# A third batch's gate stores moved ahead of the first expert's weight loads, in a kernel of causal attention and a mixture of experts

## The chip, the cores and the metric

The kernel runs as one program on one core of a Trainium2 chip. The metric is its device time in microseconds (us), the median of several runs; lower is better. Matrix products run on TensorE (PE; its weight loads are listed as PEld), element-wise work on VectorE (DVE), ScalarE (ACT) and GpSimd (POOL), and SyncE (SP) issues most of the DMA transfers. All inputs are float32 in DRAM.

## The reference

Causal attention over 4 batches, 12 heads, 448 positions and a head size of 64 gives 1792 rows ("tokens") of 768 numbers. Each token then goes through one of 8 experts, the one with the largest logit, and the result is scaled by that expert's softmax probability, the gate.

```python
scores = q @ k.T / sqrt(64)              # per batch and head, 448 x 448
attn = softmax(where(causal, scores, -1e9))
x = (attn @ v) rearranged to [1792, 768]
logits = x @ w_gate                      # [1792, 8]
e = argmax(logits, 1)
gate = softmax(logits)[token, e]
out = gate * (relu(x @ w1[e]) @ w2[e])   # w1 768 x 1024, w2 1024 x 768
```

## The kernel before

**Attention.** The work is cut into 24 pairs of heads, six to a batch. `step(p)` (L301) is one turn of a software pipeline written out by hand: it computes the scores of pair p+1 (`scores`, whose evacuation with the mask and the row minimum is VectorE's L151), their exponentials (`exps`, ScalarE), the transposes of pair p's probabilities (`transposes`), the value products of pair p-1 (`values`, whose last call copies the result from PSUM to a tile xt, L215), and `back(p-2)`. `back` multiplies xt with an identity and the pair's gate weights on TensorE (L247), scales the two heads' results by the reciprocal row sums on VectorE (L250, four products: x and its part of the logits, lgp, for each head) and stores the 128 columns of x to xd in DRAM (L227, L228, issued by SyncE). xd has 1792 rows of 784 numbers: 768 of x and 16 with the gate of the token.

**Routing.** When a batch's last pair has gone through `back`, `route(b)` (L278) is queued. It is a generator: `drip` (L263) advances it between the calls of a step, only at places that its last `yield` names; `at(j, f)` stands for the place behind call j of f. It sums the logits on GpSimd (L345 to L348), takes the maximum, computes `ex`, the exponentials of the logits, on ScalarE (L282), ranks the tokens of each expert with two small products (`rank`), turns ranks into places (`places`), and adds up a table `ids` of token numbers by expert and place (`tally`, L432). `gates(b)` (L365) turns the sum of `ex` into the gate `pre` and stores it into the last 16 columns of xd.

**Experts.** The expert stage works in 18 slots of 128 tokens of one expert. The third batch (b = B - 2) is special: its routing chooses the experts of the first three slots from three batches' tokens alone, so that the expert stage can start while the last batch's attention still runs. `top_slot` (L448) finds the expert with most tokens; SyncE reads its number (L504) and issues the eight loads of its weights (`load_raw`, L642, 768 KB each: u 0 to 3 are w1, 4 to 7 are w2). `early_slots` (L508) picks the first slot's token numbers (`pick`, L626, the cast of `idx` at L630 on GpSimd) and gathers their rows from xd (`gather`, L656, an indirect DMA on GpSimd; for an early slot it reads xd[0:1344], the first three batches). It then chooses the experts of slots 2 and 3 with small operations on VectorE and fills their entries of a table on GpSimd. The end of `route` reads the entries' numbers into registers, picks both slots' tokens and gathers the second slot's rows.

**The weights** are split into a high part (ScalarE, L695) and a low part (VectorE, L701) by `split_parts`, which then loads the next slot's part into the same buffer, or notes it as owed where that slot's expert isn't known yet. `x_turn(s)` (L720) transposes a slot's rows (TensorE, L730) and splits them too; `first` and `second` are the two products.

**The order around the change.** The calls of a step stand in `pos`; the last pair's, where the first slot's splits and transposes are mixed with the last attention work, stand in a list of their own (L1012 to L1019). Ahead of it `drip(1000)` (L1009) runs all of the routing that is left. Each engine works through its instructions in the order in which they are written, and SyncE's transfers go through one queue.

```python
def drip(n=1, at=None, among=None):
    while n and todo:
        if at and at not in (want[0] or among):
            return
```

Of the kernel before, what the change touches and what calls it, by code (L numbers as in the profile page):

```python
# [14 lines left out]
ALU = mybir.AluOpType  # L15
# [8 lines left out]
NCH = 4  # L24
# [55 lines left out]
def attention_moe_kernel(ctx: ExitStack, tc: tile.TileContext, qk_in, v_in, wi_in, w1, w2, c_in, out):  # L80
# [149 lines left out]
    def back(p):  # L230
# [17 lines left out]
        for h in (1, 0):  # L248
            for dst, lo, n in ((X[p][:, :, h], 0, D), (LG[b][:, :, 2 * pr + h], D, E)):
                nc.vector.tensor_tensor(  # L250
                    out=dst, in0=both[h][:, :, lo:lo + n],
                    in1=rs[:, :, h:h + 1].to_broadcast([C, NCH, n]), op=ALU.mult,
                )
# [9 lines left out]
    def drip(n=1, at=None, among=None):  # L263
        while n and todo:
            if at and at not in (want[0] or among):
                return
            try:
                want[0] = next(todo[0])
                n -= 1
            except StopIteration:  # L270
                todo.pop(0)
                want[0] = None
# [5 lines left out]
    def route(b):  # L278
# [3 lines left out]
        nc.scalar.activation(gt[b]["ex"], gt[b]["lg"], ACTF.Exp)  # L282
        yield at(NCH - 1, values) if b == B - 2 else at(0)
# [10 lines left out]
        if b == B - 2:  # L294
            yield from early_slots()
            for i in range(1, EARLY):
                load_regs(i)
                pick(i)
# [66 lines left out]
    def gates(b):  # L365
        g = gt[b]
        V.tensor_scalar_add(g["sm"], g["sm"], 1e-9)
# [10 lines left out]
    def places(b):  # L378
# [10 lines left out]
        V.tensor_reduce(out=g["sm"], in_=g["ex"], axis=AX.X, op=ALU.add)  # L389
# [22 lines left out]
        if b == B - 2:  # L412
            yield
            gates(b)
# [33 lines left out]
    def top_slot():  # L448
# [14 lines left out]
        def top(n, i):  # L463

            V.tensor_reduce(out=u[f"m{i}"], in_=n, axis=AX.X, op=ALU.max)
            V.scalar_tensor_tensor(out=t["eq"], in0=n, scalar=u[f"m{i}"], in1=e8_1, op0=ALU.is_equal, op1=ALU.mult)
            yield
            V.tensor_reduce(out=u[f"e{i}"], in_=t["eq"], axis=AX.X, op=ALU.min)

        def rest(n, i):  # L470
            V.tensor_scalar(out=t[f"o{i}"], in0=e8_1, scalar1=u[f"e{i}"], scalar2=None, op0=ALU.is_equal)
            yield
            V.scalar_tensor_tensor(
                out=t[f"n{i + 1}"], in0=t[f"o{i}"], scalar=float(-4 * NT), in1=n, op0=ALU.mult, op1=ALU.add
            )

# [20 lines left out]
        early["all"] = n, t, u, tf, top, rest, plus, entry  # L497
        yield from top(n, 0)
# [9 lines left out]
    def early_slots():  # L508
        n, t, u, tf, top, rest, plus, entry = early["all"]
        pick(0)  # L510
        gather(0)
        yield
        yield from rest(n, 0)
        yield from top(t["n1"], 1)
        yield from rest(t["n1"], 1)
        yield from top(t["n2"], 2)
        V.tensor_scalar(out=u["c1"], in0=u["m0"], scalar1=256.0, scalar2=None, op0=ALU.is_lt)
        V.tensor_scalar(out=u["c2"], in0=u["m0"], scalar1=384.0, scalar2=None, op0=ALU.is_lt)
# [448 lines left out]
    with tc.manual_schedule():  # L967
# [41 lines left out]
        drip(1000)  # L1009
        p = NP - 1  # L1010
        del plan[:2]
        for f, *a in [  # L1012
            (transposes, p, 0), (transposes, p, 1), (recips, p - 2), (back, p - 2), (split_parts, 0, (0,), ("low",)),
            (split_parts, 0, (1,), ("high",)), *((values, p - 1, kc) for kc in range(NCH)),
            (transposes, p, 2), (transposes, p, 3), (recips, p - 1), (back, p - 1), (split_parts, 0, (2,), ("high",)),
            (x_turn, 0), *((values, p, kc) for kc in range(NCH)), (split_parts, 0, (1,), ("low",)),
            (split_parts, 0, (3,), ("high",)), (first, 0, 0, 0), (split_parts, 0, (2,), ("low",)), (recips, p),
            (back, p), (split_parts, 0, (3,), ("low",)),
# [112 lines left out]
```

## Time and profile before

| | us |
|---|---|
| median of 3 runs | 515.77 |
| lowest and highest of them | 515.5, 517.25 |
| the profiled execution, its own time | 517.6 |
| span in that profile | 515.8 |
| TensorE busy | 490.8 (95% of the span) |
| TensorE weight loads busy | 403.0 (78%) |
| VectorE busy | 309.2 (60%) |
| ScalarE busy | 299.4 (58%) |
| GpSimd busy | 120.7 (23%) |
| mean granted clock of TensorE | 0.975 of full |

The profile is one execution, taken by the hardware profiler, with times in us from the start of its span. Its page gives busy time by engine and in 40 slices of 12.9 us, with the granted clock in tenths. The other views read the trace: the timeline lists an engine's work in order, neighbours of one kind taken together, and in brackets the idle time before and what ended it; the waits add up idle time by what was waited for; the windows give busy time, clock and DMA traffic of a stretch. A matrix product's end is modelled, and a wait for several things is put down to the one that came last.

### The profile page before, as it was taken

What the parts mean: (1) busy time and instruction counts of PE and PEld (TensorE: products, weight loads), DVE (VectorE), ACT (ScalarE), POOL (GpSimd) and SP (SyncE); (2) the same over time, 40 slices, a digit from 0 to 9 for tenths busy, and PEclk for the clock granted to TensorE, in tenths of its full rate; (3) what the DMA queues carried; (4) which work ended last, traced back from release to release, by engine and by line L of the source; (5) the groups of instructions that cost most, each with busy time, mean ns of one, the idle gap of its engine ahead of it and who ended that gap; (6) DMA issues with size and microseconds to landing.
All of it is one profiled execution on the core that took longest, in us unless ns stands there. A gap on an engine that the chain in (4) does not pass through costs nothing. (4 is left out here: it accounts for less than half of the span.)

```text
span 515.8 us, 10948 instructions
## 1 busy us (share of the span) xinstructions
PE 490.8 (95%) x3242; PEld 403.0 (78%) x3242; DVE 309.2 (60%) x872; ACT 299.4 (58%) x669; POOL 120.7 (23%) x200
## 2 busy tenths in 40 slices
PE   8999999999999489999999999999999999999973
PEld 5677766677666358989988988988899889878863
DVE  4777887787889549511025356367454314895773
ACT  6988877878778425122146347464753335775651
POOL 2000123114012164521033013113530111444201
PEclk9999999999999869999999999999999999999995
DMA  8355544445537740011382592585734257977630
GB/s 267 124 149 149 149 136 116 145 135 147 148 95 286 242 121 28 4 63 50 122 254 86 202 350 77 193 319 196 280 141 156 69 188 268 320 269 244 236 124 17
DMA packets 46327, 85.89 MB, mean 167 GB/s; under 512 B 5674, under 2 KB 18090, under 8 KB 46256
## 3 DMA queue, kind: packets, MB, share of 16 engines
q1 hardware_dynamic: 42944, 73.74, 43.2%
q0 software_dynamic: 2880, 11.13, 6.2%
q8 instruction: 29, 0.48, 0.4%
q14 instruction: 42, 0.34, 0.2%
q10 hardware_dynamic: 432, 0.20, 0.2%
HBM read 138.45 MB, written 12.70 MB: 293 GB/s over the span
## 5 line engine op out<-in xcount | busy, mean ns | idle before, releaser
L701 DVE TENSOR_TENSOR lo<-raw,hi 128x1536 fp32r<-128x1536 f32 x64 | 110.6, 1759 | 8.4 <-ACT hi L695 3.4
L163 ACT ACTIVATE s<-s,nm 66x64 f32<-66x64 f32 (+1 forms) x192 | 95.7, 501 | 21.2 <-DVE nm L151 21.1
L695 ACT CAST hi<-raw 128x1536 fp32r<-128x1536 f32 x64 | 93.7, 1485 | 9.0 <-ACTq L693 2.7
L759 ACT COPY hs<-l 128x512 f32<-128x512 f32 x36 | 21.2, 588 | 115.5 <-PE l L757 114.6
L770 PE MATMUL l<-hi,xh 128*128 128x512 f32 x216 | 86.8, 402 | 0.0
L151 DVE CUSTOM_DVE_ANT_0 s<-ps,cs 66x64 f32<-66x64 f32 (+1 forms) x192 | 70.0, 418 | 5.1 <-PE ps L145 5.0
L860 PE MATMUL y<-lo,hh 128*128 128x384 f32 x280 | 72.6, 341 | 0.1
L775 PE MATMUL l<-lo,xh 128*128 128x512 f32 x180 | 71.0, 394 | 0.6
L855 PE MATMUL y<-hi,hh 128*128 128x384 f32 x250 | 64.6, 340 | 0.4
L732 DVE TENSOR_TENSOR xl<-xT,xh 128x384 fp32r<-128x384 f32 x36 | 18.5, 552 | 76.2 <-ACT xh L731 76.1
L791 DVE SCALAR_TENSOR_TENSOR hl<-hT,hh 128x512 fp32r<-128x512 f32 x28 | 19.3, 689 | 64.8 <-ACT hh L788 36.7
L145 PE MATMUL ps<-qk 64*66 64x64 f32 (+3 forms) x384 | 56.1, 398 | 0.9 <-DVE nm L151 0.7
L863 POOL DMA_INDIRECT out<-y,idx x16 | 26.2, 1639 | 113.9 <-ACTq L693 72.3
L860 PEld LDWEIGHTS y<-lo,hh 128*128 128x128 f32 x280 | 49.7, 188 | 0.4 <-issue 0.4
L209 PEld LDWEIGHTS psx<-pt,v 128*64 128x64 f32 x384 | 26.2, 140 | 29.1 <-issue 13.0
L209 PE MATMUL psx<-pt,v 128*64 128x448 f32 (+3 forms) x384 | 48.5, 396 | 0.0
L770 PEld LDWEIGHTS l<-hi,xh 128*128 128x128 f32 x216 | 40.8, 189 | 8.2
L198 ACT COPY pt<-pst 128x512 f32<-128x512 f32 x72 | 39.7, 582 | 11.0 <-PE pst L190 10.9
L855 PEld LDWEIGHTS y<-hi,hh 128*128 128x128 f32 x250 | 44.6, 188 | 1.1 <-issue 0.7
L775 PEld LDWEIGHTS l<-lo,xh 128*128 128x128 f32 x180 | 34.0, 189 | 8.7 <-issue 1.7
L145 PEld LDWEIGHTS ps<-qk 64*128 64x128 f32 (+1 forms) x384 | 28.6, 175 | 14.3 <-issue 8.7
L788 ACT ACTIVATE hh<-hT 128x512 fp32r<-128x512 f32 x36 | 21.6, 599 | 28.4 <-PE hT L785 23.0
(162 smaller groups left out, 735.8 us busy)
## 6 DMA issues: line engine op xcount, KB each, us to landing
raw<-in_w SPq DMA_DIRECT2D x144, 768.0 KB
qk<-in_qk SPq DMA_DIRECT2D x22, 448.0 KB
v<-in_v SPq DMA_DIRECT2D x24, 256.0 KB
xd<-x SPq DMA_DIRECT2D x24, 192.0 KB
xd<-x SPq DMA_DIRECT2D x24, 32.0 KB
qk<-in_qk SPq DMA_DIRECT2D x2, 256.0 KB
qk<-in_qk SPq DMA_DIRECT2D x2, 192.0 KB
xg<-xd,idx POOLq DMA_INDIRECT x18, 5.4
```

The lines of the kernel that those rows point to most:

```text
L145: nc.tensor.matmul(ps[:m, :n], t[o, q + (S if h and q >= CUT else 0):][:, :m], t[o, k:k + n], start=True, stop=True)
L151: nc.vector.tensor_tensor_reduce(out=s[:m, h], in0=ps[:m, :n], in1=cs[:m, w:w + n], scale=-0.125, scalar=3.0e38, op0=ALU.add, op1=ALU.min, ...
L163: nc.scalar.activation(s[:m, h], s[:m, h], ACTF.Exp, bias=nm[:m, h, c:c + 1], scale=-1.0, accum_out=sm[:m, c, h:h + 1],)
L198: nc.scalar.copy(dst, src)
L209: nc.tensor.matmul(ps[D * h:D * (h + 1), kc * C:], v[:, kc, h, :], pt[:, h, o:o + n], start=(kc == 0), stop=(kc == NCH - 1),)
L695: nc.scalar.copy(parts[u][0], flat(u))
L701: nc.vector.tensor_tensor(out=lo, in0=flat(u), in1=hi.bitcast(F32), op=ALU.subtract)
L770: nc.tensor.matmul(ps, xh[:, k], wh[:, i], start=(k == 0), stop=False)
L775: nc.tensor.matmul(ps, xh[:, k], wl[:, i], start=False, stop=False)
L855: nc.tensor.matmul(y_ps[s][d], hi[:, c], wh[:, i, o], start=(h == 0 and c == 0), stop=False)
L860: nc.tensor.matmul(y_ps[s][d], hi[:, c], wl[:, i, o], start=False, stop=(h == 1 and c == 3))
L863: nc.gpsimd.indirect_dma_start(out=out, out_offset=bass.IndirectOffsetOnAxis(ap=idx[s][:, 0:1], axis=0), in_=y, in_offset=None, bounds_che ...
```

## The change

1. For the third batch, `gates` runs right behind `ex`, at the place behind `values(p, 2)`, ahead of `rank`, and no longer in `places`. Its first operation, the sum of `ex`, has moved into it from `places`, for every batch. Its stores are thereby issued before SyncE reads the first expert's number.
2. The choice for slots 2 and 3 is split between engines: the comparisons and the subtraction of the chosen expert (`o`, `n`, now two operations instead of a fused one) and the two limits (`c1`, `c2`) go to GpSimd; maximum, equality and minimum stay on VectorE. The generator stops in the middle of it (`yield at(2, values)` and `yield ()`, a place that no call has, so that only the calls of `drip` without a place go past it), and once more before the register reads.
3. Parts noted as owed for an early slot are loaded directly behind that slot's register reads. `drip` tells an empty tuple of places apart from none.
4. In `back` of pair 22 the heads are taken in the order 0, 1.
5. The list of the last pair has another order: the first low split stands ahead of `back(p - 2)`, that stands ahead of the second block of transposes, `drip(1000)` is replaced by `drip(1)` behind `back(p - 2)` and `drip(1000)` behind `x_turn(0)`, and `recips(p)` stands ahead of the last values.

```diff
@@ route
         nc.scalar.activation(gt[b]["ex"], gt[b]["lg"], ACTF.Exp)
+        if b == B - 2:
+            yield at(2, values)
+            gates(b)
         yield at(NCH - 1, values) if b == B - 2 else at(0)
         rank(b)
...
         if b == B - 2:
             yield from early_slots()
+            yield ()
             for i in range(1, EARLY):
                 load_regs(i)
+                for u in owed.pop(i, ()):
+                    load_raw(i, u)
                 pick(i)
             gather(1)
@@ drip
-            if at and at not in (want[0] or among):
+            if at and at not in (among if want[0] is None else want[0]):
@@ back
-        for h in (1, 0):
+        for h in (0, 1) if p == NP - 2 else (1, 0):
@@ gates, places
     def gates(b):
         g = gt[b]
+        V.tensor_reduce(out=g["sm"], in_=g["ex"], axis=AX.X, op=ALU.add)
         V.tensor_scalar_add(g["sm"], g["sm"], 1e-9)
...
-        V.tensor_reduce(out=g["sm"], in_=g["ex"], axis=AX.X, op=ALU.add)
         if b != B - 2:
...
-        if b == B - 2:
-            yield
-            gates(b)
         for c in range(NCH):
@@ early_slots
         pick(0)
         gather(0)
-        yield
-        yield from rest(n, 0)
-        yield from top(t["n1"], 1)
-        yield from rest(t["n1"], 1)
-        yield from top(t["n2"], 2)
-        V.tensor_scalar(out=u["c1"], in0=u["m0"], scalar1=256.0, scalar2=None, op0=ALU.is_lt)
-        V.tensor_scalar(out=u["c2"], in0=u["m0"], scalar1=384.0, scalar2=None, op0=ALU.is_lt)
+        for i in range(2):
+            o, nx, m, e = t[f"o{i}"], t[f"n{i + 1}"], u[f"m{i + 1}"], u[f"e{i + 1}"]
+            G.tensor_scalar(out=o, in0=e8_1, scalar1=u[f"e{i}"], scalar2=None, op0=ALU.is_equal)
+            G.tensor_scalar(out=nx, in0=o, scalar1=float(-4 * NT), scalar2=None, op0=ALU.mult)
+            G.tensor_tensor(out=nx, in0=nx, in1=n, op=ALU.add)
+            n = nx
+            yield () if i else at(2, values)
+            V.tensor_reduce(out=m, in_=n, axis=AX.X, op=ALU.max)
+            V.scalar_tensor_tensor(out=t["eq"], in0=n, scalar=m, in1=e8_1, op0=ALU.is_equal, op1=ALU.mult)
+            V.tensor_reduce(out=e, in_=t["eq"], axis=AX.X, op=ALU.min)
+        G.tensor_scalar(out=u["c1"], in0=u["m0"], scalar1=256.0, scalar2=None, op0=ALU.is_lt)
+        G.tensor_scalar(out=u["c2"], in0=u["m0"], scalar1=384.0, scalar2=None, op0=ALU.is_lt)
@@ the last pair
-        drip(1000)
...
-            (transposes, p, 0), (transposes, p, 1), (recips, p - 2), (back, p - 2), (split_parts, 0, (0,), ("low",)),
-            (split_parts, 0, (1,), ("high",)), *((values, p - 1, kc) for kc in range(NCH)),
-            (transposes, p, 2), (transposes, p, 3), (recips, p - 1), (back, p - 1), (split_parts, 0, (2,), ("high",)),
-            (x_turn, 0), *((values, p, kc) for kc in range(NCH)), (split_parts, 0, (1,), ("low",)),
-            (split_parts, 0, (3,), ("high",)), (first, 0, 0, 0), (split_parts, 0, (2,), ("low",)), (recips, p),
-            (back, p), (split_parts, 0, (3,), ("low",)),
+            (transposes, p, 0), (recips, p - 2), (split_parts, 0, (0,), ("low",)), (back, p - 2), (drip, 1),
+            (split_parts, 0, (1,), ("high",)), (transposes, p, 1), *((values, p - 1, kc) for kc in range(NCH)),
+            (split_parts, 0, (2,), ("high",)), (transposes, p, 2), (transposes, p, 3), (recips, p - 1), (back, p - 1),
+            (x_turn, 0), (drip, 1000), (recips, p), *((values, p, kc) for kc in range(NCH)),
+            (split_parts, 0, (3,), ("high",)), (split_parts, 0, (1,), ("low",)), (first, 0, 0, 0),
+            (split_parts, 0, (2,), ("low",)), (back, p), (split_parts, 0, (3,), ("low",)),
```

The change shows in the order of the instructions at three places.

On SyncE, from the stores of pair 18 on, the first pair of the last batch (x; tab_111 is the table with the first expert's number, raw_115 the first of the weight buffers), this stood before:

```order
L227 DMA xd<-x 64x128
L228 DMA xd<-x 128x3x128
L504 TENSOR_LOAD tab_111
L504 ISA x2
L652 ISA
L652 DMA raw_115<-in_w 128x3x512
```

The seven other loads follow in the same way, and the last of them, the stores of pair 19 and the gate's stores (pre) close the row:

```order
L652 DMA raw_122<-in_w 128x2x768
L227 DMA xd<-x 64x128
L228 DMA xd<-x 128x3x128
L227 DMA xd<-pre 64x16
L228 DMA xd<-pre 128x3x16
```

Now:

```order
L227 DMA xd<-x 64x128
L228 DMA xd<-x 128x3x128
L227 DMA xd<-pre 64x16
L228 DMA xd<-pre 128x3x16
L496 TENSOR_LOAD tab_111
L496 ISA x2
L650 ISA
L650 DMA raw_115<-in_w 128x3x512
```

The two stores of pre have moved from behind the eight weight loads and pair 19's stores to ahead of the read of the expert's number.

On VectorE, at the end of step 20, around the copy of pair 19's xt (the L151 rows ahead of it evacuate pair 21's scores, those behind it pair 22's), before:

```order
L151 ISA s,nm<-ps,cs 128x320
L151 ISA nm 128x1
L215 COPY xt<-psx 128x448
L151 ISA s,nm<-ps,cs 66x64
L151 ISA nm 66x1
```

Now:

```order
L151 ISA s,nm<-ps,cs 128x320
L151 ISA nm 128x1
L373 TENSOR_REDUCE sm<-ex 128x4
L374 TENSOR_SCALAR sm<-sm 128x4
L375 RECIPROCAL sm<-sm 128x4
L215 COPY xt<-psx 128x448
L151 ISA s,nm<-ps,cs 66x64
L151 ISA nm 66x1
```

The three operations on sm stand ahead of the copy; they stood further down, behind the ranks.

On VectorE, where the last pair's list begins (psb is pair 21's product, the xt behind it pair 22's, raw_115 the first weight part; m, e, n and c are the small tiles of the choice), before:

```order
L466 SCALAR_TENSOR_TENSOR eq<-n_2381,m_2384,cs 21x8
L468 TENSOR_REDUCE e_2387<-eq 21x1
L517 TENSOR_SCALAR c_2388<-m_2382 21x1
L518 TENSOR_SCALAR c_2389<-m_2382 21x1
L222 TENSOR_SCALAR rs<-sums 128x8
L223 RECIPROCAL rs<-rs 128x8
L250 TENSOR_TENSOR x<-psb,rs 128x4x64
L250 TENSOR_TENSOR lgp<-psb,rs 128x4x8
L250 TENSOR_TENSOR x<-psb,rs 128x4x64
L250 TENSOR_TENSOR lgp<-psb,rs 128x4x8
L701 TENSOR_TENSOR lo<-raw_115,hi 128x1536
L215 COPY xt<-psx 128x448
```

Now:

```order
L222 TENSOR_SCALAR rs<-sums 128x8
L223 RECIPROCAL rs<-rs 128x8
L699 TENSOR_TENSOR lo<-raw_115,hi 128x1536
L250 TENSOR_TENSOR x<-psb,rs 128x4x64
L250 TENSOR_TENSOR lgp<-psb,rs 128x4x8
L250 TENSOR_TENSOR x<-psb,rs 128x4x64
L250 TENSOR_TENSOR lgp<-psb,rs 128x4x8
L512 TENSOR_REDUCE m_2390<-n_2387 21x1
L513 SCALAR_TENSOR_TENSOR eq<-n_2387,m_2390,cs 21x8
L514 TENSOR_REDUCE e_2393<-eq 21x1
L215 COPY xt<-psx 128x448
```

The low split of the first part has moved ahead of pair 21's four products, the choice of the third slot behind them, and c is no longer VectorE's.

## Rows read from the trace of the kernel before

**Rows 1.** The page's 40 slices: TensorE's busy share and granted clock in tenths.

```profile
PE   8999999999999489999999999999999999999973
...
PEclk9999999999999869999999999999999999999995
```

**Rows 2.** Windows: us, busy PE, PEld, DVE, ACT, POOL (x), PE clock, DMA share, GB/s.

```profile
175.00:180.00 5.00, 0.00 (x0) 0.00 (x0) 0.66 (x4) 0.00 (x0) 1.14 (x1) 0.57 0.27 56
...
185.00:190.00 5.00, 5.00 (x22) 2.93 (x19) 2.36 (x4) 2.99 (x3) 2.94 (x7) 0.56 0.29 59
```

**Rows 3.** Waits from 150 to 215: total us, times, longest us.

```profile
POOL xg L659 <- DMA xd<-x: 14.5, 1, 14.5
```

**Rows 4.** Timeline of GpSimd, first slot: start, us, engine, line, operation, [idle before].

```profile
164.21 0.19 POOL L630 CAST idx<-ids 128x1 int32 x1 [1.35 <-DVE ids L432]
178.86 1.25 POOL L659 DMA_INDIRECT xg<-xd,idx  x1 [14.46 <-DMA xd<-x]
```

**Rows 5.** Timeline of SyncE's queue: the weight loads and the gate's second store.

```profile
156.42 6.43 SPq L652 DMA_DIRECT2D raw<-in_w  x8
...
167.37 0.82 SPq L228 DMA_DIRECT2D xd<-pre  x1
```

**Rows 6.** Windows, as in rows 2: the weight loads, and a later gather.

```profile
164.00:175.00 11.00, 9.96 (x96) 6.62 (x94) 10.12 (x39) 8.46 (x16) 0.19 (x1) 1.00 1.05 389
...
420.50:428.80 8.30, 8.30 (x43) 7.28 (x42) 1.57 (x3) 4.02 (x4) 1.07 (x2) 1.00 1.01 366
```

**Rows 7.** Timeline of TensorE, last two pairs and the first slots' transposes.

```profile
170.16 1.95 PE L209 MATMUL psx<-pt,v 128*64 128x448 f32 x16
183.09 1.54 PE L730 MATMUL xT<-cs,xg 128*128 128x128 f32 x6 [8.48 <-DMA xg<-xd,idx]
184.56 3.68 PE L209 MATMUL psx<-pt,v 128*64 128x448 f32 x16
...
190.97 1.12 PE L247 MATMUL psb<-wi,xt 64*128 64x72 f32 x16
...
198.77 0.82 PE L730 MATMUL xT<-cs,xg 128*128 128x128 f32 x6
```

**Rows 8.** Waits of TensorE from 191 to the end, the largest.

```profile
PE y L903 <- DVE lo L701: 2.1, 2, 1.4
```

**Rows 9.** Timeline of GpSimd: the second slot's chain and gather, and a later one.

```profile
180.14 0.21 POOL L519 TENSOR_TENSOR d<-e,e 21x1 f32<-21x1 f32 x1
...
187.52 1.14 POOL L659 DMA_INDIRECT xg<-xd,idx  x1 [0.58 <-POOL idx L630]
...
428.75 1.23 POOL L723 COPY gate<-xg 128x1 f32<-128x1 f32 x1 [7.23 <-DMA xg<-xd,idx]
```

**Rows 10.** Timeline of all engines: the attention loop, a reciprocal, the first low split.

```profile
152.05 0.62 DVE L215 COPY xt<-psx 128x448 f32<-128x448 f32 x1 [0.33 <-PE psx L209]
...
152.80 0.21 ACT L282 ACTIVATE ex<-lg 128x32 f32<-128x32 f32 x1
152.86 0.22 DVE L151 CUSTOM_DVE_ANT_0 s<-ps,cs 66x64 f32<-66x64 f32 x1 [0.19 <-PE ps L145]
...
153.15 0.29 PEld L145 LDWEIGHTS ps<-qk 64*128 64x128 f32 x2 [0.24 <-DVE nm L151]
...
160.18 0.18 DVE L368 RECIPROCAL sm<-sm 128x4 f32<-128x4 f32 x1
...
171.15 1.75 DVE L701 TENSOR_TENSOR lo<-raw,hi 128x1536 fp32r<-128x1536 f32 x1
```

**Rows 11.** View of the tile xg: its 18 gathers.

```profile
DMA to landing us min/median/max: 3.8/5.4/8.6
```

**Rows 12.** Timeline: GpSimd's sum of logits in two batches, and VectorE beside the later.

```profile
143.11 0.59 POOL L345 TENSOR_TENSOR l<-lgp 128x192 f32<-128x192 f32 x1 [19.51 <-DVE lgp L250]
...
193.52 3.82 DVE L701 TENSOR_TENSOR lo<-raw,hi 128x1536 fp32r<-128x1536 f32 x2
193.69 2.03 POOL L345 TENSOR_TENSOR l<-lgp 128x192 f32<-128x192 f32 x1 [2.21 <-DVE lgp L250]
```

More of the change, by code (lines that the diff above doesn't have):

```diff
@@ L461, in top_slot @@
         tf = small.tile([N, 8], F32, tag="f_tab", name="tf", bufs=1)
-        def top(n, i):
-            V.tensor_reduce(out=u[f"m{i}"], in_=n, axis=AX.X, op=ALU.max)
-            V.scalar_tensor_tensor(out=t["eq"], in0=n, scalar=u[f"m{i}"], in1=e8_1, op0=ALU.is_equal, op1=ALU.mult)
-            yield
[L468 to L475, printed above, removed]
         def plus(out, c, d, f):
@@ L495, in entry @@
             G.tensor_copy(tf[:, o + 2:o + 3], c)
-        early["all"] = n, t, u, tf, top, rest, plus, entry
-        yield from top(n, 0)
+        early["all"] = n, t, u, tf, plus, entry
+        V.tensor_reduce(out=u["m0"], in_=n, axis=AX.X, op=ALU.max)
+        V.scalar_tensor_tensor(out=t["eq"], in0=n, scalar=u["m0"], in1=e8_1, op0=ALU.is_equal, op1=ALU.mult)
+        yield
+        V.tensor_reduce(out=u["e0"], in_=t["eq"], axis=AX.X, op=ALU.min)
         V.tensor_scalar(out=tab0[:, 0:1], in0=u["e0"], scalar1=float(E), scalar2=None, op0=ALU.add)
@@ L508, in early_slots @@
     def early_slots():
-        n, t, u, tf, top, rest, plus, entry = early["all"]
+        n, t, u, tf, plus, entry = early["all"]
         pick(0)
         gather(0)
-        yield
-        yield from rest(n, 0)
-        yield from top(t["n1"], 1)
-        yield from rest(t["n1"], 1)
-        yield from top(t["n2"], 2)
-        V.tensor_scalar(out=u["c1"], in0=u["m0"], scalar1=256.0, scalar2=None, op0=ALU.is_lt)
-        V.tensor_scalar(out=u["c2"], in0=u["m0"], scalar1=384.0, scalar2=None, op0=ALU.is_lt)
+        for i in range(2):
[10 more added lines that the diff above has]
+        G.tensor_scalar(out=u["c2"], in0=u["m0"], scalar1=384.0, scalar2=None, op0=ALU.is_lt)
         G.tensor_tensor(out=u["d1"], in0=u["e1"], in1=u["e0"], op=ALU.subtract)
```

## The prediction

> **What bounds the kernel now.** I read the page first: its 40 slices show TensorE busy nearly everywhere, with one hole behind a third of the span, and a granted clock that is full on both sides of it and falls there [rows 1]. The views by stretch give the hole its size: nothing on TensorE from 175 to 180, and a granted clock of 0.57 of full speed there and 0.56 from 185 to 190, which is mostly the lower of its two levels, 1.2 GHz instead of 2.4 [rows 2]. TensorE had stood idle before it fell. Then the list of waits: GpSimd's gather of the first slot's rows waited 14.5 us for a store to xd [rows 3], though its indices were ready at 164.4 [rows 4]. The view names that store by its tile only; the code says which one it is. The gather reads rows 0 to 1343 of xd. The x stores of pairs 18 and later write rows from 1344 on, and those of pair 17 and earlier are long through. What is left is the third batch's gates (`pre`), whose second store SyncE issued at 167.37, behind eight weight loads of 768 KB each, issued from 156.42 on [rows 5]. The DMA engines work at full share through all of 164 to 175 [rows 6]; a small store behind 6 MB in the same queue is through when the loads are. So the gather starts at 178.86 [rows 4], and TensorE, done with pair 22 at 174.6, stands for 8.48 us until the rows arrive, at 183.09 [rows 7]. Behind this place TensorE is the bound up to the end: from 191 on its longest group of waits sums to 2.1 us [rows 8]. What is gained here should therefore reach the end nearly whole.
>
> **The change, term by term.** The profiled execution took 517.6 us with a span of 515.8; the three runs have a median of 515.77, so that execution is 1.8 us long. I take the differences from its trace and lay them on the median.
>
> *Stores ahead of the loads.* SyncE now issues both gate stores before it reads the first expert's number, at about 154, into a queue with little in it, and the gather's last condition becomes its indices. With the shift of the loop (below) these are ready at 165.6, and a gather starts some 0.6 us behind its indices (the second slot's did [rows 9]): 166.2. It now runs beside the weight loads. Without them it took 4.2 us (178.86 to 183.09 [rows 4, 7]). A later gather, at a DMA share of 1.01, as here [rows 6], was waited for 7.2 us from the end of its issue [rows 9]; with an issue of 1.25 [rows 4] that is 8.5. So the rows land between 170.4 and 174.7; I take the upper end, since the load is the same. TensorE will want them at about 176.4 (below). The idle 8.48 us go: **-8.5**. The two stores take about 1 us of issue on SyncE, in time in which it waits for the expert's number; were that cover gone, the weights would start 1 us later, and the splits that read them have more than that in hand.
>
> *The clock.* Without the idle stretch the clock should stay up. At the lower level six transposes took 1.54 us against 0.82 later, and sixteen value matmuls 3.68 against 1.95 [rows 7]: 2.45 less by these alone. A mean of 0.56 from 185 to 190 [rows 2] means half speed until about 189.4; half of the time from 183.09 to there would be 3.1. I take **-2.8**, with 2.45 and 3.1 as ends.
>
> *The gates' three VectorE operations in the attention loop.* They now stand in front of a copy to xt, and the first reads `ex`, which ScalarE makes only at 152.80, behind the exponentials of that step; VectorE did the copy at 152.05 [rows 10]. It will now start the gates' sum at 153.05, and three operations of 0.2 us each (the reciprocal is one [rows 10]) put the copy at about 153.55. The score evacuation behind it had waited 0.19 us for TensorE, so it goes from 152.86 to 154.1. TensorE's next scores already waited for that evacuation (at 153.15 [rows 10]); then come the transposes, the exponentials and so on round the loop, which has no slack that I can find: **+1.2**, from 0.9 (some slack that I don't see; two of the operations are gone from a later step) to 1.5.
>
> *The last pair's order.* The first low split, 1.75 us [rows 10], goes ahead of pair 21's four products; these free the banks for pair 23's later transposes, and the copy of pair 22's xt comes behind them. Against that, eight small VectorE operations on [21 x 8] or [21 x 1] go, and TensorE does pair 21's back product before a block of transposes. Following each queue through with its old durations, I get TensorE ready for the slot's transposes 0 to 1.4 us later than at 174.6; the upper end holds if the first of the new round trips between GpSimd and VectorE keeps VectorE waiting. I take **+0.6**. With the shift of 1.2: 176.4.
>
> *The second slot's rows.* GpSimd's chain from the differences of the experts to the second gather took 7.4 us (180.14 to 187.52 [rows 9]). It will start when the third slot's expert is known, behind the low split and pair 21's products: about 174. That gives a gather at 181.6, and with the median 5.4 us to landing rows at 187.0, with the longest, 8.6, at 190.2 [rows 11]. TensorE took them at 198.77 [rows 7]; with the gain it asks at about 189.4. **+0.4**, from 0 to 1.5.
>
> *At no cost:* the operations moved to GpSimd lie in time in which it waited for the store; the second expert's first load, now owed and issued behind its register reads, comes some 1 us later relative to TensorE, which reads it only after the whole first slot; ScalarE's casts and copies, in their new order, have idle time before each use.
>
> Sum: -8.5 - 2.8 + 1.2 + 0.6 + 0.4 = -9.1, so 515.8 - 9.1 = **506.7 us**. The bounds together run from -10.7 to -6.5: 505.1 to 509.3.
>
> **Rivals.** *A, GpSimd held up by the low splits.* GpSimd's first sum of the logits took 0.59 us in one batch and 2.03 in a later one, where two low splits, 3.82 us in all, ran on VectorE beside it [rows 12]. In the new order the index copies and the second gather meet the second and third low split, about 180 to 184. If they are held for both, the gather starts at 185.5, the rows land at 190.9 to 194.1, and TensorE waits 1.5 to 4.7 us instead of 0.4: a gain of 4.8 to 8, at the middle 6.4, so 509.4. Against it: by my times most of the chain is over before these splits begin. Chance 0.10. The Trainium skill (SBUF — State Buffer, Who interferes with whom) states a lock: of a VectorE operation with two SBUF inputs and a GpSimd operation that reads SBUF, the later one is blocked for the other's whole length. This speaks against moving work to GpSimd near the splits, and by that rule the time would be this rival's, if the two meet. The trace agrees with the lock (2.03 against 0.59); whether they meet, no row of before shows.
>
> *B, the first gather lands late.* If it gets through only when the weights are done, that is at about 176.5 now [rows 2], 1.2 later with the shift, 1.0 more for its own 0.4 MB (128 rows of 784 numbers) at 389 GB/s [rows 6], and a tail, then at about 179.5. So 3.1 us of idle time remain, and with a second fall of the clock its 2.8 are lost again: 509.8 to 512.6, the likeliest 511. For it: it shares the DMA engines with most of the loads. Against it: the later gather got through in the same load [rows 9]. Chance 0.09.
>
> *C, slower.* The gather is still held by a store behind the loads, so that the change does not do what it says. Place: the x stores of pairs 19 to 22 stay behind the weights in SyncE's queue. If one of them is among the gather's conditions, the idle stretch and the low clock stay, and the delays of the loop, 1.2, and of the last pair, 0.6, come on top: 517.6 us. It decides where the gather starts no earlier than 178.9. Against it: those rows lie outside of what the gather reads. Chance 0.03.
>
> **How the numbers follow.** Main case 0.78, A 0.10, B 0.09, C 0.03. The predicted time is the main case's, whose own range is 505.1 to 509.3. Taking in the middle of A and the near edge of B, and leaving out the rest above, I give 505.0 to 510.3. About 0.3% (1.5 us) is what a measurement of this kernel can tell from no change; main, A and nearly all of B lie below 514.2. Faster 0.94, within it 0.03 (the far edge of B, with a longer delay of the loop), slower 0.03.
>
> **What would show it.** In the changed kernel's profile: the gate stores issued at about 154, ahead of eight weight loads that start near 157.6; the first gather at about 166 instead of 178.86, with no long wait before it; TensorE's slices without the hole, and a granted clock of 1.00 from 170 to 195; the value matmuls of pair 23 in about 1.95 us. VectorE should stand for over 1 us before the gates' sum near 153, and the steps behind it should lie 1.2 us later than now. Pair 23's back product should start near 181.5 instead of 190.97 [rows 7]. Rival A would show as a TensorE wait for the second slot's rows near 189, B as a shorter wait before the first slot's transposes, C as the old wait of GpSimd. I would be wrong in the main point if the hole were closed and the end did not move with it: then something behind 200, which I take to follow TensorE, is held by something else.

## The result, and the profile after

The change takes the kernel from 515.63 us (median of 4 runs, 514.33 to 517.25) to 508.37 us (4 runs, 507.6 to 510.66), a ratio of 0.9865 with a 95% interval of 0.9822 to 0.9908. Timed once more in a later comparison it took 506.94 us against 514.99, a ratio of 0.9853 (0.9827 to 0.988). The forecast was 506.7, with a range of 505.0 to 510.3. The profiled execution took 508.84 us with a span of 507.0: between the two traces lie 8.8 us.

TensorE's busy share and its granted clock on the page of the changed kernel, in 40 slices of 12.7 us:

```profile
PE   8999999999999999999999999999999999999983
...
PEclk9999999999998999999999999999999999999997
```

The hole behind a third of the span [rows 1] is gone. One slice ahead of its place the clock is a little lower, 8 tenths, which it was not before. SyncE's queue in the timeline of the changed kernel:

```profile
154.23 0.45 SPq L227 DMA_DIRECT2D xd<-pre  x1
154.73 0.58 SPq L228 DMA_DIRECT2D xd<-pre  x1
157.88 6.12 SPq L650 DMA_DIRECT2D raw<-in_w  x8
```

Both gate stores go out ahead of the loads; before, the second went out at 167.37 [rows 5]. GpSimd's timeline, with the first slot's indices and gather, and the second slot's:

```profile
166.90 0.19 POOL L628 CAST idx<-ids 128x1 int32 x1 [1.14 <-DVE ids L435]
168.12 1.25 POOL L657 DMA_INDIRECT xg<-xd,idx  x1 [1.04 <-DMA raw<-in_w]
...
171.77 1.73 POOL L509 TENSOR_TENSOR n<-n,n 21x8 f32<-21x8 f32 x1
...
180.89 3.24 POOL L628 CAST idx<-ids 128x1 int32 x2 [0.67 <-issue]
184.28 1.14 POOL L657 DMA_INDIRECT xg<-xd,idx  x1 [0.15 <-POOL idx L628]
```

The wait of 14.5 us for a store [rows 3, 4] has become one of 1.04 us. The row at 171.77, a subtraction of the choice, comes up again below. The view of the DMA issues gives the time from issue to landing, for a window around the first gather and one around the second:

```profile
xg<-xd,idx POOLq DMA_INDIRECT x1, 7.6
...
xg<-xd,idx POOLq DMA_INDIRECT x1, 4.1
```

So the first slot's rows land at 175.7, the second's at 188.4. TensorE's timeline, first of the kernel before, pair 19's and pair 20's value products, which [rows 7] do not hold:

```profile
150.05 1.95 PE L209 MATMUL psx<-pt,v 128*64 128x448 f32 x16
...
157.92 1.95 PE L209 MATMUL psx<-pt,v 128*64 128x448 f32 x16
```

and then of the changed kernel, from the same place on:

```profile
150.30 1.95 PE L209 MATMUL psx<-pt,v 128*64 128x448 f32 x16
...
154.60 0.59 PE L145 MATMUL ps<-qk 64*128 64x192 f32 x2 [1.14 <-DVE nm L151]
155.12 2.82 PE L190 MATMUL pst<-cs,s 128*128 128x128 f32 x12
...
160.97 1.95 PE L209 MATMUL psx<-pt,v 128*64 128x448 f32 x16
...
177.09 0.87 PE L728 MATMUL xT<-cs,xg 128*128 128x128 f32 x6
178.14 1.95 PE L209 MATMUL psx<-pt,v 128*64 128x448 f32 x16 [0.18 <-PE xT L728]
...
182.29 1.11 PE L247 MATMUL psb<-wi,xt 64*128 64x72 f32 x16
...
190.08 0.82 PE L728 MATMUL xT<-cs,xg 128*128 128x128 f32 x6
```

The transposes of the first slot start at 177.09 with no wait, 1.4 us after their rows landed, and pair 23's value products take 1.95 us instead of 3.68. The second slot's transposes come at 190.08 instead of 198.77. The new idle time is the 1.14 us at 154.60, and the twelve transposes behind it take 2.82 us. What TensorE waits for there stands in VectorE's timeline:

```profile
153.30 0.19 DVE L373 TENSOR_REDUCE sm<-ex 128x4 f32<-128x32 f32 x1 [1.32 <-ACT ex L282]
...
153.82 0.59 DVE L215 COPY xt<-psx 128x448 f32<-128x448 f32 x1
154.33 0.21 DVE L151 CUSTOM_DVE_ANT_0 s<-ps,cs 66x64 f32<-66x64 f32 x1
```

VectorE stands 1.32 us for ScalarE's ex. Counted from pair 19's value products, the copy comes 1.5 us later than before and the score evacuation 1.2 us [rows 10], as forecast. What was not forecast is the clock behind it, in the windows of the changed kernel (us, then busy PE, PEld, DVE, ACT, POOL, granted clock, DMA share, GB/s):

```profile
152.50:155.00 2.50, 1.36 (x11) 0.91 (x10) 1.60 (x10) 0.77 (x5) 0.24 (x1) 1.00 0.03 5
155.00:157.50 2.50, 2.50 (x13) 2.38 (x12) 1.48 (x11) 0.96 (x2) 1.05 (x5) 0.52 0.12 12
157.50:160.00 2.50, 2.50 (x27) 2.02 (x27) 1.06 (x3) 2.23 (x10) 0.00 (x0) 0.80 0.36 59
```

From 155 to 157.5 the clock is 0.52 of full, nearly all of it the lower level, 1.2 GHz. Before, there was neither idle time nor a lower clock here:

```profile
155.00:157.50 2.50, 2.50 (x28) 1.95 (x28) 2.07 (x11) 2.45 (x10) 0.72 (x4) 1.00 0.01 2
```

The gain can be read off one stretch of TensorE, from the start of pair 19's value products (150.05 before, 150.30 after) to the start of the second slot's transposes (198.77 and 190.08): 48.72 us before, 39.78 after, 8.94 less. The rest of the program, taken together, is 0.1 us longer. The experiments are compared by this stretch, since it leaves out what varies from one execution to the next at the head and at the tail. It still holds what the clock does in that execution.

### The profile page after: what moved, and what is told of

It is laid out like the page before. It is cut to its first block, busy times and chain, and to the rows that moved or that the text cites. A ratio compares the mean times of both kernels' runs of the same rounds, so it can differ in the third digit from the quotient of the medians.

```text
span 507.0 us, 10946 instructions
## 1 busy us (share of the span) xinstructions
PE 489.3 (97%) x3242; PEld 402.5 (79%) x3242; DVE 307.7 (61%) x866; ACT 299.4 (59%) x669; POOL 123.2 (24%) x208
## 5 line engine op out<-in xcount | busy, mean ns | idle before, releaser
L151 DVE CUSTOM_DVE_ANT_0 s<-ps,cs 66x64 f32<-66x64 f32 (+1 forms) x192 | 69.9, 418 | 5.3 <-PE ps L145 5.2
L209 PE MATMUL psx<-pt,v 128*64 128x448 f32 (+3 forms) x384 | 46.8, 386 | 0.2 <-PE xT L728 0.2
L190 PE MATMUL pst<-cs,s 128*128 128x128 f32 x288 | 39.0, 284 | 0.0
```

Of the source, the lines that this page charges most:

```text
L151: nc.vector.tensor_tensor_reduce(out=s[:m, h], in0=ps[:m, :n], in1=cs[:m, w:w + n], scale=-0.125, scalar=3.0e38, op0=ALU.add, op1=ALU.min, ...
L190: nc.tensor.transpose(ps[:, i * C:(i + 1) * C], pr_t[p, qc][:, h, o:o + C], ident)
L209: nc.tensor.matmul(ps[D * h:D * (h + 1), kc * C:], v[:, kc, h, :], pt[:, h, o:o + n], start=(kc == 0), stop=(kc == NCH - 1),)
```

## The experiments

| | median us | ratio to before (95%) | loop | ready | stretch |
|---|---|---|---|---|---|
| before | 514.34 to 515.63 | | 7.87 | 24.55 | 48.72 |
| the change | 508.37 | 0.9865 (0.9822 to 0.9908) | 10.67 | 26.79 | 39.78 |
| the change, again | 506.94 | 0.9853 (0.9827 to 0.988) | 9.08 | 25.19 | 38.22 |
| stores alone | 506.71 | 0.9841 (0.9801 to 0.988) | 9.08 | 25.60 | 38.79 |
| rest alone | 520.63 | 1.0104 (1.0063 to 1.0144) | 7.87 | 40.40 | 53.40 |
| gates one step later | 503.86 | 0.9783 (0.9751 to 0.9815) | 7.87 | 24.00 | 37.02 |
| half the loads | 507.84 | 0.986 (0.9821 to 0.99) | 7.87 | 24.55 | 40.79 |
| ex one place earlier | 504.17 | 0.9801 (0.9783 to 0.9818) | 7.87 | 23.98 | 36.98 |
| old rest, gates one step later | 504.22 | 0.9799 (0.9781 to 0.9816) | 7.86 | 24.38 | 37.57 |
| choice on VectorE | 504.5 | 0.9807 (0.9788 to 0.9825) | 7.87 | 24.46 | 37.47 |
| old list | 504.27 | 0.9797 (0.9776 to 0.9817) | 7.87 | 24.29 | 37.45 |
| rest alone, choice on VectorE | 514.28 | 0.9993 (0.9977 to 1.0009) | 7.87 | 24.89 | 47.38 |
| choice behind the copy | 503.82 | 0.9783 (0.9759 to 0.9807) | 7.87 | 23.75 | 36.76 |

Each ratio is to runs of the kernel before in the same comparison; their medians are the 514.34 to 515.63 of the first row. All three columns at the right are differences of start times in the profiled execution's timeline, counted from pair 19's value products: *loop* to pair 20's value products, *ready* to the first slot's transposes (less the wait for their rows, where there is one), *stretch* to the second slot's transposes. The rest alone has no such wait: its idle time lies ahead of pair 21's products.

**1. The stores alone.** The kernel before, with the gates moved as in the change and nothing else (the sum of `ex` moves with them; those lines are left out here):

```diff
         nc.scalar.activation(gt[b]["ex"], gt[b]["lg"], ACTF.Exp)
+        if b == B - 2:
+            yield at(2, values)
+            gates(b)
...
-        if b == B - 2:
-            yield
-            gates(b)
```

> The kernel before with part 1 of the change alone: the third batch's gates run behind ex and their stores go ahead of the weight loads; choice and last pair as before. Theory (the order of the stores makes the whole gain; the trace of the change shows the loop 2.8 us late because VectorE waits for ex, TensorE stands 1.14 us and its clock falls for some us): the first gather starts near 168, the hole is gone, TensorE takes the first slot's rows near 177.4 and the end lies 8.4 us ahead of before, from 7.5 to 9.2, as in the change. Rival (the new order of the last pair and the choice on GpSimd carry part of it): a gain of 6 us or less, with a wait of over 1 us for the first or the second slot's rows.

It has all of the gain that the medians resolve: 506.71 us, a gather at 167.24, transposes at 176.61 without a wait, a stretch of 38.79 us. So the order of the stores is enough, and the rival falls. TensorE in this run:

```profile
151.01 1.95 PE L209 MATMUL psx<-pt,v 128*64 128x448 f32 x16
...
155.31 0.59 PE L145 MATMUL ps<-qk 64*128 64x192 f32 x2 [1.15 <-DVE nm L151]
155.83 1.53 PE L190 MATMUL pst<-cs,s 128*128 128x128 f32 x12
...
160.09 1.95 PE L209 MATMUL psx<-pt,v 128*64 128x448 f32 x16
```

Its idle time is the change's, 1.15 us, but the twelve transposes behind it take 1.53 us instead of 2.82: here the clock did not fall, and the loop took 9.08 us, 1.2 longer than before.

**2. The rest alone.** The changed kernel with its gates put back behind the ranks, and so its stores behind the loads:

```diff
-        if b == B - 2:
-            yield at(2, values)
-            gates(b)
...
+        if b == B - 2:
+            yield
+            gates(b)
         for c in range(NCH):
```

> The changed kernel with its gates, and so their stores, put back to where they were, behind the weight loads; choice on GpSimd, owed loads and last pair as in the change. Theory: the first gather starts near 178.9 again, TensorE stands until 183, and the time is that of before within 1 us, since a better last pair only makes the idle stretch longer. Rival (the new order carries part of the gain): 2 to 3 us under the time of before.

A miss, for theory and rival both: 520.63 us, some 6 us slower than before. The wait in VectorE's timeline, ahead of the choice's maximum:

```profile
182.60 0.15 DVE L512 TENSOR_REDUCE m<-n 21x1 f32<-21x8 f32 x1 [14.14 <-POOL n L509]
...
183.11 0.60 DVE L215 COPY xt<-psx 128x448 f32<-128x448 f32 x1
```

GpSimd's:

```profile
180.35 1.25 POOL L657 DMA_INDIRECT xg<-xd,idx  x1 [14.83 <-DMA xd<-x]
...
182.38 0.19 POOL L509 TENSOR_TENSOR n<-n,cnt 21x8 f32<-21x8 f32 x1
```

And TensorE's:

```profile
183.77 1.99 PE L247 MATMUL psb<-wi,xt 64*128 64x72 f32 x16 [14.45 <-DVE xt L215]
```

The choice's first operations now stand on GpSimd behind the held gather; VectorE waits for their result; the copy of pair 21's xt stands behind that on VectorE, and TensorE waits for the copy, with the rest of the attention behind it. Before, the gather held up only itself and what GpSimd did next.

**3. The gates one step later.** The changed kernel, with the three operations behind the next score evacuations, where ex has long been there:

```diff
-        if b == B - 2:
-            yield at(2, values)
-            gates(b)
         yield at(NCH - 1, values) if b == B - 2 else at(0)
         rank(b)
         yield at(0) if b == B - 2 else at(1)
+        if b == B - 2:
+            gates(b)
         yield from places(b)
```

> The changed kernel with one thing moved: the gates' three VectorE operations stand one step later, behind the next score evacuations and the reciprocals, still ahead of the read of the first expert's number. Theory (it is the wait for ex that costs, 1.14 us of idle TensorE and then some 1.6 us at the lower clock): no idle time on TensorE near 153.5, a granted clock of 1.00 through 155 to 160, and 2.3 to 2.8 us less than the change, 505.7, with a wait of up to 0.5 us for the first slot's rows, which land only 1.4 us ahead of their use in the change. Rival (the three operations cost wherever they stand on VectorE, or the first gather is what then ends last): within 1 us of the change, 507.4 to 509.4, with a wait for the rows in the second case.

The loop is back at 7.87 us, the clock stays, and the stretch is 37.02 us, 2.76 less than in the profile of the change: the theory's size, 2.3 to 2.8. Its window, to set beside the change's:

```profile
155.00:157.50 2.50, 2.50 (x29) 2.03 (x29) 2.28 (x14) 2.50 (x10) 1.25 (x6) 1.00 0.12 11
```

The rows' margin didn't shrink: everything that leads to the gather came earlier too. At 503.86 us this beats both kernels; the 505.7 expected was counted from the change's first median, and from its second, 506.94, it is 3.1 us less.

**4. Half the loads.** The kernel before, with w2's four loads behind the gate's stores:

```diff
-        for i in range(8):
+        for i in range(4):
             load_raw(0, i)
...
             gates(b)
+            for i in range(4, 8):
+                load_raw(0, i)
```

> The kernel before with four of the first expert's eight weight loads ahead of the gate's stores, and the other four (w2) right behind them. Theory (the stores wait for the bytes ahead of them in the queue): 3.1 MB less at 389 GB/s are 8.1 us, so the first gather starts near 170.8 instead of 178.86, and TensorE's idle stretch shrinks from 8.5 to between 0 and 5 us, the latter if the rows then come through the other four loads as late as 179.3: 504.5 to 512. Rival (the gather is held by something that does not scale with the loads): the gather stays at 178.9 and the time at that of before.

The gather, and TensorE's wait for its rows:

```profile
170.09 1.25 POOL L661 DMA_INDIRECT xg<-xd,idx  x1 [5.21 <-DMA raw<-in_w]
```

```profile
176.91 1.47 PE L732 MATMUL xT<-cs,xg 128*128 128x128 f32 x6 [1.82 <-DMA xg<-xd,idx]
```

The gather starts 8.8 us earlier (9.3, counted from pair 19's value products), against 8.1 worked out from the bytes: with half of the loads ahead of the stores, most of the wait is gone, 5.21 us instead of 14.46. The view names a weight load as what ended it. The gather doesn't read one; that it was the gate's store rests on the start time and on experiment 1. The rows came through the other four loads in 6.8 us, and 1.82 us of idle time were left. The clock fell behind them, for the next products took 2.99 us instead of 1.95:

```profile
178.31 2.99 PE L209 MATMUL psx<-pt,v 128*64 128x448 f32 x16
```

**5. ex one place earlier.** The changed kernel; ScalarE makes ex right behind the logits' subtraction, ahead of that step's exponentials:

```diff
-        nc.scalar.activation(gt[b]["ex"], gt[b]["lg"], ACTF.Exp)
+        if b != B - 2:
+            nc.scalar.activation(gt[b]["ex"], gt[b]["lg"], ACTF.Exp)
...
+        if b == B - 2:
+            nc.scalar.activation(g["ex"], g["lg"], ACTF.Exp)
         V.scalar_tensor_tensor(out=g["oh"], in0=g["lg"], scalar=0.0, in1=own, op0=ALU.is_equal, op1=ALU.mult)
```

> The changed kernel with one instruction moved: ScalarE computes the third batch's ex one place earlier, ahead of the exponentials of that step; the gates stay where the change put them. Theory (VectorE's wait for ex is what costs, the three operations hardly): VectorE doesn't wait before the gates' sum, TensorE's wait for the evacuation behind falls from 1.14 to 0.3 to 0.6 us, the clock stays up, and from the start of pair 19's value products to the second slot's transposes it takes 37.3 to 37.8 us (the change 39.8, the run with the gates one step later 37.0): a time near 504.5. Rival (it is the three operations ahead of the copy): TensorE still waits about 1 us there, and the time is 506 to 508.5.

Better than expected: no wait at all, and a loop of 7.87 us. VectorE:

```profile
151.72 0.18 DVE L376 TENSOR_REDUCE sm<-ex 128x4 f32<-128x32 f32 x1
...
152.23 0.59 DVE L215 COPY xt<-psx 128x448 f32<-128x448 f32 x1
```

The three operations now fill time in which VectorE waited for pair 19's products (0.33 us in [rows 10]), and cost nothing. So it was the wait for ex that cost.

**6 to 8. What the rest of the change is worth.** Three runs take apart what is left once nothing waits for ex. The first is the kernel before with the gates moved as in experiment 3.

> The kernel before with the gates moved one step later than in the change, but ahead of the weight loads as there; choice, owed loads and last pair as before. Theory (the rest of the change gains 0.6 us once nothing waits for ex: the run with the stores alone took 38.8 us from pair 19's value products to the second slot's transposes, 1.2 of it the wait for ex): 37.6 us for that stretch against 37.0, and a time of 504.4. Rival (the rest of the change gains nothing or costs, as I predicted with 0.6): 36.4 to 37.0 us, and 503.3 to 503.9.

The second is experiment 3 with the choice's operations back on VectorE (the same for c1 and c2):

```diff
-            G.tensor_scalar(out=o, in0=e8_1, scalar1=u[f"e{i}"], scalar2=None, op0=ALU.is_equal)
-            G.tensor_scalar(out=nx, in0=o, scalar1=float(-4 * NT), scalar2=None, op0=ALU.mult)
-            G.tensor_tensor(out=nx, in0=nx, in1=n, op=ALU.add)
+            V.tensor_scalar(out=o, in0=e8_1, scalar1=u[f"e{i}"], scalar2=None, op0=ALU.is_equal)
+            V.tensor_scalar(out=nx, in0=o, scalar1=float(-4 * NT), scalar2=None, op0=ALU.mult)
+            V.tensor_tensor(out=nx, in0=nx, in1=n, op=ALU.add)
```

> The run with the gates one step later, with the moved operations of the choice (three for each slot and the two limits) back on VectorE at the same places in the order. Theory (VectorE is close to the path in the last pairs, and eight operations of some 0.15 to 0.2 us stand ahead of copies to xt for which TensorE waits already): pair 21's and pair 22's products wait 0.4 to 0.6 us longer each, and the stretch takes 37.6 to 38.2 us instead of 37.0. Rival (the choice costs nothing on either engine): 37.0 within 0.2.

The third is experiment 3 with the last pair's list of the kernel before, `drip(1000)` ahead of it and the old order of heads.

> The run with the gates one step later, with the last pair's list, the place of its last routing and the order of heads as before; the choice stays on GpSimd. Theory (the list and the choice gain about the same): 37.2 to 37.6 us for the stretch; the second slot's gather starts earlier than in the change's list, since its picks stand ahead of the first slot's gate copy. Rival (the list is all of the gain, and GpSimd's answers come late in the old one): 37.8 us or more, with VectorE waiting over 0.5 us for GpSimd's n ahead of a copy to xt.

The stretch is 37.57 us with both old, 37.45 with the new choice alone, 37.47 with the new list alone and 37.02 with both. Each without the other gains 0.1, together they gain 0.55: 0.1% of the time, which these runs' medians don't resolve. The stretch does, as far as single traces go: less their 1.21 us of a longer loop, experiments 1 and 9 give 37.58 and 37.01, where the same kernels with the gates one step later gave 37.57 and 37.02. The second run stayed at the low edge of its expected 37.6 to 38.2: the eight operations lengthen one wait only, the one ahead of pair 21's products, from 0.39 us to

```profile
169.15 1.11 PE L247 MATMUL psb<-wi,xt 64*128 64x72 f32 x16 [0.85 <-DVE xt L215]
```

**9. The change again.** The changed kernel as it is, with a second profile.

> The changed kernel itself once more, on one chip with the run in which its choice comes behind the copy. Open is what the 1.14 us of idle TensorE near 154 cost: in the change's profile the granted clock then fell for some 3 us and the loop lost 2.8 us, in the run with the stores alone the same wait was there, the clock stayed and the loop lost 1.2. Theory (the fall is not certain, it comes in some executions): 506.2 to 508.5 over the runs, mean clocks between 0.990 and 0.995, and from the start of pair 19's value products to pair 20's 9.1 us (no fall) or up to 10.7 (fall). Rival (something else in the change, on GpSimd or in the last pair, makes the fall): 10.7 us again, and every run near 0.990.

This time the loop took 9.08 us and the clock stayed, with the same idle 1.14 us:

```profile
155.00:157.50 2.50, 2.32 (x18) 1.96 (x18) 2.03 (x17) 1.11 (x3) 0.67 (x3) 1.00 0.12 14
```

So the fall comes in some executions only, and the rival is out. The profiled execution was the fastest of the five; what the clock did in the others at this place, no trace shows. The five runs took 505.85 to 508.16 us and had mean clocks of 0.988 to 0.995, both a little under the expected bands.

**10. The rest alone, with the choice on VectorE.** Experiment 2 with the edit of experiment 7.

> The run with the rest of the change alone (stores behind the loads, 520.6 us), with the moved operations of the choice back on VectorE. Theory (it lost 6 us because the choice on GpSimd stands behind the held gather, VectorE waits 14.1 us for its n, and the copy to xt, and so TensorE, wait behind it): VectorE's wait is gone, TensorE stands once, about 8 us, before the first slot's transposes, and the time is that of before, 514.5, within 1 us. Rival (the new list costs it): 518 or more.

514.28 us: the 6 us of experiment 2 are gone, and TensorE waits where it did before, by its list of waits and its timeline:

```profile
PE xT L728 <- DMA xg<-xd,idx: 8.4, 1, 8.4
```

```profile
183.38 1.54 PE L728 MATMUL xT<-cs,xg 128*128 128x128 f32 x6 [8.36 <-DMA xg<-xd,idx]
184.85 2.65 PE L209 MATMUL psx<-pt,v 128*64 128x448 f32 x16
...
197.51 0.82 PE L728 MATMUL xT<-cs,xg 128*128 128x128 f32 x6
```

That settles experiment 2: the loss was GpSimd's place in the chain, not the list. It also says that the new list by itself gains nothing that the medians resolve while the gather is held. Its stretch, 47.38 us, is still 1.34 less than that of before; the part on the prediction takes this up.

**11. The choice behind the copy.** Experiment 3, with the second slot's maximum, equality and minimum behind pair 21's copy to xt:

```diff
-            yield () if i else at(2, values)
+            yield () if i else at(NCH - 1, values)
```

> The run with the gates one step later, with the second slot's maximum, equality and minimum behind pair 21's copy to xt instead of ahead of it. Theory (the three operations, 0.6 us, hold that copy, for which TensorE waits 0.39 us ahead of pair 21's products): that wait is gone and the stretch from pair 19's value products to the second slot's transposes falls from 37.0 to about 36.7 us; the time, 503.6, can't be told from 503.9. Rival (the products then wait for something else, or the low split that now starts later holds pair 21's products back): 37.0 us or more.

Pair 21's products start without a wait, at 169.14, and the stretch is 36.76 us, as expected. The time, 503.82 us, can't be told from that of experiment 3; both are the fastest here.

## Why the prediction was right

**The main case happened**, and the time lay inside its range. Its terms, against the two traces:

| term | forecast | measured |
|---|---|---|
| idle time ahead of the first slot | -8.5 | -8.48, all of it gone |
| clock behind it, and the second slot's rows | -2.8 + 0.4 | -2.69 (first to second slot's transposes: 15.68 before, 12.99 after) |
| the gates in the attention loop | +1.2 | +2.80 (7.87 before, 10.67 after) |
| the last pair's order, and the gates' operations gone from its steps | +0.6 | -0.56 (ready less loop: 16.68 before, 16.12 after) |
| sum | -9.1 | -8.9 |

The sum is closer than its parts deserve: two errors of over 1 us, the clock in the loop and the last pair, cancelled. That is luck.

**The stores.** The first slot's gather, landing and use came in the order worked out, at 168.1, 175.7 and 177.1 us instead of 166.2, 174.7 and 176.4; the low clock in the loop makes up most of the gather's delay. From the issue the first rows took 7.6 us, between the 4.2 of the lone gather and the 8.5 that I took as upper end. That the loads ahead of it held the store is shown by experiment 1, and experiment 4 with half of them agrees.

**The clock behind the idle time.** The term stands at -2.8 and came out at -2.69 against the trace of before, but that trace had more of the low clock than most: its mean clock was 0.975, those of the 15 executions of before in the last comparison 0.980 to 0.986. In experiment 10, with nearly the same idle time (8.36 us), pair 23's value products took 2.65 us instead of 3.68, and from the first to the second slot's transposes it took 14.13 us instead of 15.68, some 0.2 of it by the new list (13.19 in experiment 6, 13.02 in experiment 3). The step "I take the differences from its trace and lay them on the median" took the whole of -2.8 off a median that, by this, likely held less of it. No second trace of the kernel before is there to show how much.

**The gates in the loop.** The step "+1.2, from 0.9 to 1.5" was right for the wait and left out the clock. In the trace the forecast rests on, TensorE had a clock of 1.00 in this part of the loop, and I priced only the delay. The wait costs 1.2 us by itself (experiments 1 and 9, where the loop took 9.08) and 2.8 where the clock falls behind it (the profile of the change). Of the three traces with this wait, one has the fall and two do not. The Trainium skill (TensorE: Matmul & The Clock Gate, Part 1: The HAM clock gate) says of the clock's rise that its moment varies between executions of one kernel; these traces show such a variation for the fall.

**The last pair.** The step "ready 0 to 1.4 us later" had the wrong sign. Its upper end supposed that the first round trip between GpSimd and VectorE keeps VectorE waiting; that costs next to nothing, since GpSimd's three operations run while VectorE does score evacuations. In the trace of before TensorE waits 0.22 us for pair 21's copy and 0.39 us for pair 22's; in the trace of the change 0.38 and nothing. Of the 0.56, 0.16 came with the gates' operations gone from these steps: in experiment 6, which has the old rest, ready less loop is already 16.52. Experiment 3, with the new rest, has 16.13, another 0.39 less. Over the whole stretch the rest is worth the 0.55 us of experiments 6 to 8. The order of heads and the owed loads were not tried by themselves.

**The second slot's rows.** "+0.4" was too much, for TensorE did not wait. The gather started later than forecast, and its rows landed sooner behind it, in 4.1 us, against the 5.4 to 8.6 of the forecast. It started not at 181.6 but at 184.28, since GpSimd was held up: two index copies took 3.24 us together, where one took 0.19 [rows 4]. VectorE's low splits ran beside them, as one did beside the subtraction at 171.77, which took 1.73 us:

```profile
170.16 0.19 POOL L509 TENSOR_TENSOR n<-n,cnt 21x8 f32<-21x8 f32 x1
171.73 1.72 DVE L699 TENSOR_TENSOR lo<-raw,hi 128x1536 fp32r<-128x1536 f32 x1
...
180.67 3.42 DVE L699 TENSOR_TENSOR lo<-raw,hi 128x1536 fp32r<-128x1536 f32 x2
```

That is rival A's mechanism. It is also the Trainium skill's lock (SBUF — State Buffer, Who interferes with whom), with which these rows agree. But its price was nothing: the rows landed 4.1 us later, at 188.4, and TensorE asked at 190.08. The rival's sum took a gather 1.2 us later and the slower landings of other gathers.

**Rivals B and C** did not come: the first rows had 1.4 us to spare, and no store behind the loads held the gather. Experiment 4 shows B's shape, 1.82 us of wait with half of the loads issued at the wrong time.

**The medians.** The forecast laid the sum on a median of 515.8. The medians moved by 7.3 us in the first comparison and by 8.1 in the second, the profiles by 8.8. So the agreement of 8.9 with 9.1 is one between two single executions. As a ratio, the forecast of 0.9824 lies just inside the first interval and just outside the second: the gain was forecast 1.0 to 1.8 us too large.

## What to carry to other kernels

A small store that others wait for belongs ahead of large loads in a queue, by issue order: look for a long wait on a DMA whose own size is small, and count the bytes issued ahead of it. Before work is moved to an idle engine, ask what that engine is held by: an engine that waits for a transfer passes its wait on to whoever needs its next result, so that the same move cost 6 us with the store late and gained at most half a microsecond with the store early. Where an operation is put in front of a loop's critical copy, look up when its input is made, not only how long it takes: here the three operations cost nothing, and the wait for their input between 1.2 and 2.8 us.

## What the runs showed of the hardware

In the profile of the change TensorE stood 1.14 us, and behind that its granted clock was 0.52 from 155 to 157.5 and 0.80 from 157.5 to 160, which cost another 1.6 us. The same wait in two other executions (1.14 and 1.15 us, experiments 9 and 1) left it at 1.00. What decides between the two, no run here shows. In experiment 4 it fell behind 1.82 us. I had counted on a fall behind the 8.48 us of before and the 3.1 us of rival B, and on none behind the wait in the loop.

Small GpSimd operations met VectorE's low splits at several places: the subtraction of the second choice took 1.73 us, that of the first, ahead of the split, 0.19. In the trace of the change none of it reached TensorE: its two waits from 171 to 190 are 0.38 us for a copy of VectorE's and 0.18 us for its own transposes.

The first gather starts 1.04 us behind its indices in each run with the stores early, where the second slot's took 0.58 [rows 9]. The view puts the 1.04 down to a weight load, which the gather doesn't read; what it is stays open.
